# Two heads as one unit in a decode attention kernel: three slots of 64 KB a partition in place of five of 32 KB

## The chip, the core and the metric

The kernel runs on one core of a Trainium2 chip. The core has a matrix engine (PE, with its weight loads shown as PEld), a vector engine (DVE), an activation engine (ACT), GpSimd (POOL) and a queue engine (SP), and 16 DMA engines that move data between HBM and the on-chip SBUF of 128 partitions. Matrix products land in PSUM. The metric is the device time of one execution in microseconds.

## The reference

One decode step of a transformer block for B = 2 sequences, D = 512, H = 32 heads of 128 columns, a cache of 8192 keys and values for each head, and a gated feed-forward part of F = 1792. Everything is float32.

```python
q = layernorm(x) @ wq                       # (2, 1, 512) @ (512, 4096), split into 32 heads
scores = einsum("bhqd,bhkd->bhqk", q, k_cache) * 128 ** -0.5
p = softmax(scores)
o = einsum("bhqk,bhkd->bhqd", p, v_cache)
h = x + concat_heads(o) @ wo                # (4096, 512)
y = layernorm(h)
out = h + (silu(y @ w_gate) * (y @ w_up)) @ w_down
```

k_cache and v_cache hold 268 MB each, and all else is small beside them: each byte is used once, with one query row for each head and sequence.

## The kernel before

**Work.** A unit is one head of one sequence, i = 0 to 63 (head `i // 2`, sequence `i % 2`). Its K is 8192 x 128 floats, 4 MB, laid out so that partition p holds 64 consecutive keys, one run of 32 KB. The scores are made on DVE: `mult` (L245) multiplies half of K, 128 x 4096, in place by the query row, and `reduce` (L248) adds over the 128 columns; two such pairs make a unit. `local_max` (L256) takes the largest score of a partition, `spread_max` (L260) turns the 128 of them into a row on PE, and `softmax`, called one unit later between the first `mult` and the first `reduce`, takes the largest of that row on DVE (L264), brings it to all partitions with a PE product and an ACT copy (L266, L268), takes the exponential with its row sums on ACT (L271) and sums them over the partitions on PE (L275). `recip` follows between the second pair. `pv` (L288) multiplies p by V: 16 products of 128 x 512, each on a 32-column strip of PE, four strips in turn; in the trace each is two matrix instructions. `epilogue` (L301, L304, L311) copies the four strips out of PSUM, adds them with weights 1/denominator and stores one column of `oT`.

**Slots and the load queue.** One pool of five slots of 32 KB a partition (`RING = 5`) holds everything that is loaded: K units, V units, wq and wo in four groups of eight heads each (2 MB a group), and at the end w_gate, w_up and w_down. `order` is the list of all loads; `pump` issues them in that order on SP, each as soon as the item five places before it in the list has been marked `used`. On the chip a load waits at the head of SP's queue for the last reader of its slot, and the loads behind it wait with it. `after[i]` says which V units are multiplied during K unit i: the lag between K and V grows from one unit to five (`LEAD`, `STEP`). w_q's next group is projected (`project_q`, L223) every 16 units, and wo's group is applied (`project_o`, L318) after each 16.

**Order of the work.** `manual_schedule` keeps the program's order on each engine. In a unit, PE runs the two softmax products of the unit before (L266, L275), then `pv` of the V unit that is due, then `spread_max`, then the epilogue.

Of the kernel before, what the change touches and what calls it, by code (L numbers as in the profile page):

```python
# [8 lines left out]
F32 = mybir.dt.float32  # L9
# [5 lines left out]
RING = 5  # L15
# [4 lines left out]
def tile_decode_block(  # L20
# [16 lines left out]
    assert DH == P and B == 2 and D == 512 and F == 14 * P  # L37
# [3 lines left out]
    NJ = S // P  # L41
    FINE = 16
    NCH = NJ // FINE
    G = 8
    NG = H // G
    NP = B * H
    LEAD = 4
    STEP = 12
# [3 lines left out]
    NW = NJ // W  # L52

# [3 lines left out]
    ring = ctx.enter_context(tc.tile_pool(name="ring", bufs=RING))  # L57
# [10 lines left out]


    def k_pieces(i):  # L70
        return NCH if i == 0 else 1

    def v_pieces(i):
        return NCH if i == NP - 1 else 1

    def pieces(kind, i):
        n = k_pieces(i) if kind == "k" else v_pieces(i)
        return [((kind, i), e * (NJ // n), NJ // n) for e in range(n)]


    after = []
    for i in range(NP):
        upto = i - 1 - min(LEAD, i // STEP)
        after.append(list(range(sum(map(len, after)), upto + 1)))
    rest = list(range(sum(map(len, after)), NP))

    order = [(("wq", 0), 0, 1)]

    def stream_v(i):
        if i == NP - 2:  # L90
            order.append((("wo", NG - 1), 0, 1))
        order.extend(pieces("v", i))
        if (i + 1) % (B * G) == 0 and i + 1 < NP:
            order.append((("wo", i // (B * G)), 0, 1))

    for i in range(NP):
        g, r = divmod(i + 2, B * G)
        if r == 0 and g < NG:
            order.append((("wq", g), 0, 1))
        order.extend(pieces("k", i))  # L100
        for v in after[i]:
            stream_v(v)
    for v in rest:
        stream_v(v)
    order += [(("wg", 0), 0, DC)] + [(("wu", 0), c, n) for c, n in ((0, 2), (2, 1), (3, 1))]
    order += [(("wd", 0), c, n) for c, n in ((0, 4), (4, 4), (8, 3), (11, 2), (13, 1))]
    items = list(dict.fromkeys(o[0] for o in order))
# [4 lines left out]
    def load(item, e, n):  # L112
        if item not in slot:
            slot[item] = ring.tile([P, NJ * DH], F32, name="ring")
        t = slot[item]
        kind, i = item
        if kind in "kv":
            src = k_cache if kind == "k" else v_cache
            h, b = divmod(i, B)
            nc.sync.dma_start(  # L120
                t[:, e * DH : (e + n) * DH],
                src[b, h].rearrange("(p j) d -> p (j d)", p=P)[:, e * DH : (e + n) * DH],
            )
        elif kind == "wq":
            nc.sync.dma_start(
                t[:, : DC * G * DH].rearrange("p (c m) -> p c m", c=DC),
                wq[:, i * G * DH : (i + 1) * G * DH].rearrange("(c p) m -> p c m", p=P),
            )
        elif kind == "wo":
            nc.sync.dma_start(  # L130
                t[:, : G * D].rearrange("p (c m) -> p c m", c=G),
                wo[i * G * DH : (i + 1) * G * DH, :].rearrange("(c p) m -> p c m", p=P),
            )
        elif kind in ("wg", "wu"):
            src = w_gate if kind == "wg" else w_up
            nc.sync.dma_start(
                t[:, e * F : (e + n) * F],
                src.rearrange("(p c) f -> p (c f)", p=P)[:, e * F : (e + n) * F],
            )
        else:  # L140
            nc.sync.dma_start(
                t[:, e * D : (e + n) * D],
                w_down.rearrange("(p c) m -> p (c m)", p=P)[:, e * D : (e + n) * D],
            )

    def pump():
        while state["next"] < len(order):
            piece = order[state["next"]]
            if piece[0] not in slot:
                n = items.index(piece[0])  # L150
                if n >= RING and items[n - RING] not in done:
                    return
# [11 lines left out]
    ones = const.tile([P, P], F32, name="ones")  # L164
    nc.vector.memset(ones, 1.0)
    nscale = const.tile([1, P], F32, name="nscale")
    nc.vector.memset(nscale, -SCALE)
    mhalf = const.tile([B, 1], F32, name="mhalf")
    nc.vector.memset(mhalf, -0.5)
    opart = []  # L170
    for n in range(2):
# [3 lines left out]

    diag = const.tile([P, W], F32, name="diag")
    nc.vector.tensor_reduce(
        diag, ident.rearrange("p (t r) -> p r t", t=4)[:, :W, :], axis=AX.X, op=OP.add
    )
# [8 lines left out]
    def layernorm(src, runs):  # L188
# [8 lines left out]
        y = work.tile([B, D], F32, name="ln_y")  # L197
        nc.vector.tensor_scalar(y, src, mv[:, 0:1], rstd, op0=OP.subtract, op1=OP.mult)
        yt = psum.tile([P, DC, B], F32, name="small", bufs=3)
        for c in range(DC):  # L200
            cols = y.rearrange("b (p c) -> b c p", c=DC) if runs else y.rearrange("b (c p) -> b c p", c=DC)
            nc.tensor.transpose(yt[:, c, :], cols[:, c, :], ident[:B, :B])
# [3 lines left out]
    xT_ps = layernorm(xs, False)  # L206
    xT = const.tile([P, DC, B], F32, name="xT")
    nc.vector.tensor_copy(xT, xT_ps)
    xb = const.tile([P, DC * B, P], F32, name="xb")
    nc.vector.tensor_copy(  # L210
        xb, xT.rearrange("p c b -> p (c b)")[:, :, None].to_broadcast([P, DC * B, P])
    )

    qsb = {}

    def project_q(g):
        w = slot[("wq", g)][:, : DC * G * DH].rearrange("p (c m) -> p c m", c=DC)
        qsb[g] = work.tile([P, B, G * DH], F32, name="qsb")
        for b in range(B):
            for n in range(0, G * DH, 512):  # L220
                ps = psum.tile([P, 512], F32, name="wide", bufs=2)
                for c in range(DC):
                    nc.tensor.matmul(  # L223
                        ps,
                        xb[:, c * B + b, :],
                        w[:, c, n : n + 512],
                        start=(c == 0),
                        stop=(c == DC - 1),
                    )
                nc.scalar.activation(qsb[g][:, b, n : n + 512], ps, AF.Copy)  # L230
        used(("wq", g))
# [6 lines left out]
    def mult(i, j0, n):  # L238
        h, b = divmod(i, B)
        g, hh = divmod(h, G)  # L240
# [3 lines left out]
        qb = qsb[g][:, b, hh * DH : (hh + 1) * DH][:, None, :].to_broadcast([P, n, DH])  # L244
# [17 lines left out]
    def softmax(i):  # L262
        gm = work.tile([1, 1], F32, name="gm")
        nc.vector.tensor_reduce(gm, st[i]["mrow"], axis=AX.X, op=OP.max)  # L264
        nb_ps = psum.tile([P, 1], F32, name="small", bufs=3)
        nc.tensor.matmul(nb_ps, nscale, gm, start=True, stop=True)  # L266
        nb = work.tile([P, 1], F32, name="nb")
        nc.scalar.activation(nb, nb_ps, AF.Copy)  # L268
        st[i]["p"] = work.tile([P, NJ], F32, name="p", bufs=LEAD + 4)
        rs = work.tile([P, 1], F32, name="rs")  # L270
        nc.scalar.activation(  # L271
            st[i]["p"], st[i]["s"], AF.Exp, bias=nb, scale=SCALE, accum_out=rs
        )
        st[i]["den"] = psum.tile([P, 1], F32, name="small", bufs=3)
        nc.tensor.matmul(st[i]["den"], ones, rs, start=True, stop=True)  # L275

    def recip(i):
        r = work.tile([P, 1], F32, name="r")
        nc.vector.reciprocal(r, st[i]["den"])  # L279
        st[i]["r"] = work.tile([P, W], F32, name="rdiag", bufs=LEAD + 4)  # L280
        nc.scalar.activation(st[i]["r"], diag, AF.Copy, scale=r)  # L281

    def pv(i, j0, n):
        vt = slot[("v", i)]
        o = opart[i % 2]
        for w in range(j0 // W, (j0 + n) // W):
            t = w % 4
            nc.tensor.matmul(  # L288
                o[32 * t : 32 * t + W, :],
                st[i]["p"][:, w * W : (w + 1) * W],  # L290
# [7 lines left out]
    def epilogue(i):  # L298
        h, b = divmod(i, B)
        osb = work.tile([P, W * DH], F32, name="osb")  # L300
        nc.scalar.activation(osb, opart[i % 2], AF.Copy)  # L301
        ot_ps = psum.tile([P, 1], F32, name="small", bufs=3)
        for a in range(W):
# [3 lines left out]
                st[i]["r"][:, a : a + 1],  # L307
# [3 lines left out]
        nc.scalar.activation(oT[:, h, b : b + 1], ot_ps, AF.Copy)  # L311
        del st[i]

    def project_o(h0, h1):
        g = h0 // G
        w = slot[("wo", g)][:, : G * D].rearrange("p (c m) -> p c m", c=G)
        for h in range(h0, h1):
            nc.tensor.matmul(  # L318
                attn, oT[:, h, :], w[:, h - g * G, :], start=(h == 0), stop=(h == H - 1)
            )  # L320
        if h1 % G == 0:
            used(("wo", g))

    def values(v):
        pv(v, 0, NJ)

    def outputs(v):
        epilogue(v)
        if (v + 1) % (B * G) == 0 and v + 1 < NP:
            project_o((v + 1) // B - G, (v + 1) // B)  # L330

    project_q(0)
    for i in range(NP):
        n = FINE if k_pieces(i) > 1 else 2 * FINE
        for c, j0 in enumerate(range(0, NJ, n)):
            mult(i, j0, n)
            if i:
                if c == 0:
                    softmax(i - 1)
                if c == 1:  # L340
                    recip(i - 1)
            reduce(i, j0, n)
            if c == 1:
                for v in after[i]:
                    values(v)
        if (i + 1) % (B * G) == 0 and i + 1 < NP:
            project_q((i + 1) // (B * G))
        local_max(i)

        if i == NP - 1:  # L350
            for v in after[i]:
                outputs(v)
            for v in rest[:2]:
                values(v)
                outputs(v)
        spread_max(i)
        if i < NP - 1:
            for v in after[i]:
                outputs(v)
    softmax(NP - 1)  # L360
    warm = const.tile([1, 1], F32, name="warm")
    nc.scalar.activation(warm, mhalf[:1, :], AF.Sigmoid)
    recip(NP - 1)
    for v in rest[2:-1]:
        values(v)
        outputs(v)
        if v == NP - 3:
            project_o(H - G, H - 1)
    for j0 in range(0, NJ, FINE):
        pv(NP - 1, j0, FINE)  # L370
    epilogue(NP - 1)
    project_o(H - 1, H)


    h1 = const.tile([B, D], F32, name="h1")
    nc.vector.tensor_add(h1, attn, xs)  # L376
    hT_ps = layernorm(h1, True)
# [99 lines left out]
```

## Time and profile before

| | us |
|---|---|
| median of 3 runs | 1319.63 (1319.53 to 1319.73) |
| the profiled execution, its own time | 1319.64 |
| its span | 1317.8 |
| DVE busy | 1156.5 |
| PE busy | 662.0 |
| PE weight loads busy | 255.4 |
| ACT busy | 117.2 |

The span runs from the first instruction to the last; the execution's own time is 1.84 us longer. A group of instructions is given by line, engine, operation and tiles, with its count, busy time, mean duration and the idle time of its engine just before it. A DMA issue is shown with the median time from issue to landing. In the rows by time, the columns are start, duration, engine, line, operation, tiles, and in brackets the idle time before with what ended it; "SPq" is the queue engine issuing a load. In the rows by window the columns are the window, its length, the busy time (and number of instructions) of PE, PEld, DVE, ACT and POOL, PE's granted clock as a share of full speed, the busy share of the DMA engines, and GB/s.

### The profile page before, as it was taken

The page shows a single profiled execution, that of the slowest core. Times are in us where ns is not written, and L with a number is a line of the kernel's source. Part 1 is how long each engine was busy: PE and PEld are TensorE (multiplying, and loading weights), DVE is VectorE, ACT ScalarE, POOL GpSimd, SP SyncE. Part 2 cuts the span into 40 slices and gives each one's busy share as a digit, 9 for nine tenths or more (in the row PEclk, how much of TensorE's full clock was granted, in tenths as well). Part 3 has the DMA queues.
Part 4 walks back from the last instruction along what each step waited for, and adds up shares of the span by engine and source line. Part 5 has one row for each costly group of instructions (what it writes and reads, how often), then busy time and mean ns, then how long its engine had stood idle before and what let it go on. Part 6 is the DMA issues. An engine that isn't in the chain of part 4 may idle for free.

```text
span 1317.8 us, 8050 instructions
## 1 busy us (share of the span) xinstructions
PE 662.0 (50%) x3328; PEld 255.4 (19%) x3328; DVE 1156.5 (88%) x474; ACT 117.2 (9%) x404; POOL 1.9 (0%) x9
## 2 busy tenths in 40 slices
PE   5444444257554434535753444442644753444586
PEld 2121111113211111211321122111212211111122
DVE  6999999997999999989889999997799999999601
ACT  1001000001000000000100000000100000100010
POOL 0000000000000000000000000000000000000000
PEclk9666656567675756666767656656857756665677
DMA  9999999999999999999999999999999999999997
GB/s 402 438 433 428 430 437 435 422 439 432 428 433 437 433 430 430 436 432 434 429 430 430 435 436 430 433 429 434 436 430 429 432 430 431 437 435 431 429 425 334
DMA packets 26921, 565.19 MB, mean 429 GB/s; under 512 B 2426, under 2 KB 2434, under 8 KB 9220
## 3 DMA queue, kind: packets, MB, share of 16 engines
q1 hardware_dynamic: 26872, 564.67, 99.7%
q8 instruction: 26, 0.43, 0.1%
q14 instruction: 11, 0.09, 0.0%
q10 hardware_dynamic: 12, 0.01, 0.0%
HBM read 564.66 MB, written 0.00 MB: 428 GB/s over the span
## 4 chain that ended last, share of the span: by engine, by line
DVE 47%; DMA 45%; PE 7%; issue 0%; ACT 0%; SPq 0%; DVEq 0%
DMA ring<-in_A_k_cache_dram 31%; DVE s L248 24%; DVE ring L245 23%; DMA ring<-in_A_v_cache_dram 11%; PE wide L223 4%; DMA ring<-in_B_w_down_dram 2%; PE opart L288 2%; PE attn L318 1%; DMA ring<-in_A_wq_dram 1%; DVE m L256 0%; PE small L425 0%; PE small L304 0%; DVE r L279 0%; PE small L260 0%; DVE gm L264 0%
## 5 line engine op out<-in xcount | busy, mean ns | idle before, releaser
L245 DVE TENSOR_TENSOR ring<-ring,qsb 128x4096 f32<-128x4096 f32 (+1 forms) x130 | 565.5, 4350 | 69.6 <-DMA ring<-in_A_k_cache_dram 57.7
L248 DVE TENSOR_REDUCE s<-ring 128x32 f32<-128x4096 f32 (+1 forms) x130 | 565.1, 4347 | 0.7 <-DVE gm L264 0.5
L288 PE MATMUL opart<-ring,p 128*4 128x512 f32 x2048 | 356.3, 858 | 110.1 <-DMA ring<-in_A_v_cache_dram 110.1
L260 PE MATMUL small<-ident,m 128*1 128x128 f32 x128 | 31.7, 341 | 270.9 <-DVE m L256 270.9
L266 PE MATMUL small<-gm,nscale 1*128 1x1 f32 x128 | 35.9, 347 | 203.6 <-DVE gm L264 203.6
L288 PEld LDWEIGHTS opart<-ring,p 128*4 128x4 f32 x2048 | 58.3, 108 | 349.2 <-issue 232.6
L304 PE MATMUL small<-rdiag,osb 128*128 128x1 f32 x512 | 98.1, 313 | 7.1 <-ACT osb L301 7.1
L304 PEld LDWEIGHTS small<-rdiag,osb 128*128 128x128 f32 x512 | 92.7, 271 | 32.4 <-issue 18.7
L266 PEld LDWEIGHTS small<-gm,nscale 1*128 1x128 f32 x128 | 30.5, 294 | 213.5 <-DVE gm L264 210.8
L260 PEld LDWEIGHTS small<-ident,m 128*1 128x1 f32 x128 | 5.5, 81 | 329.2 <-DVE m L256 327.0
L275 PE MATMUL small<-rs,ones 128*128 128x1 f32 x128 | 36.2, 352 | 47.0 <-ACT p L271 47.0
L223 PE MATMUL wide<-ring,xb 128*128 128x512 f32 x128 | 58.2, 614 | 3.1 <-DMA ring<-in_A_wq_dram 3.1
L281 ACT ACTIVATE rdiag<-diag,r 128x4 f32<-128x4 f32 x64 | 19.0, 297 | 452.3 <-DVE r L279 452.3
L264 DVE TENSOR_REDUCE gm<-small 1x1 f32<-1x128 f32 x64 | 17.4, 272 | 35.1 <-PE small L260 35.1
L301 ACT ACTIVATE osb<-opart 128x512 f32<-128x512 f32 x64 | 37.8, 590 | 92.3 <-PE opart L288 92.3
L275 PEld LDWEIGHTS small<-rs,ones 128*128 128x128 f32 x128 | 30.8, 298 | 52.4 <-ACT p L271 52.4
L268 ACT ACTIVATE nb<-small 128x1 f32<-128x1 f32 x64 | 10.9, 171 | 286.0 <-PE small L266 285.6
L318 PE MATMUL attn<-ring,oT 128*2 128x512 f32 x64 | 36.2, 726 | 0.3 <-ACT oT L311 0.3
L311 ACT ACTIVATE oT<-small 128x1 f32<-128x1 f32 x64 | 11.0, 171 | 279.1 <-PE small L304 279.1
L223 PEld LDWEIGHTS wide<-ring,xb 128*128 128x128 f32 x128 | 24.8, 196 | 35.8 <-issue 35.8
L376 DVE TENSOR_TENSOR h<-attn,xs 2x512 f32<-2x512 f32 x1 | 0.7, 679 | 29.2 <-PE attn L318 29.2
L271 ACT ACTIVATE p<-s,nb 128x64 f32<-128x64 f32 x64 | 22.2, 348 | 2.1
(43 smaller groups left out, 88.4 us busy)
## 6 DMA issues: line engine op xcount, KB each, us to landing
ring<-in_A_k_cache_dram SPq DMA_DIRECT2D x63, 4096.0 KB, 32.4
ring<-in_A_v_cache_dram SPq DMA_DIRECT2D x63, 4096.0 KB, 30.5
ring<-in_A_wq_dram SPq DMA_DIRECT2D x4, 2048.0 KB, 26.0
ring<-in_A_wo_dram SPq DMA_DIRECT2D x4, 2048.0 KB, 27.0
ring<-in_A_k_cache_dram SPq DMA_DIRECT2D x4, 1024.0 KB, 12.3
ring<-in_A_v_cache_dram SPq DMA_DIRECT2D x4, 1024.0 KB, 23.0
ring<-in_B_w_gate_dram SPq DMA_DIRECT2D x1, 3584.0 KB, 33.5
ring<-in_B_w_down_dram SPq DMA_DIRECT2D x2, 1024.0 KB, 27.4
```

Source lines behind the costliest of these rows:

```text
L223: nc.tensor.matmul(ps, xb[:, c * B + b, :], w[:, c, n : n + 512], start=(c == 0), stop=(c == DC - 1),)
L245: nc.vector.tensor_tensor(kt, kt, qb, op=OP.mult)
L248: nc.vector.tensor_reduce(st[i]["s"][:, j0 : j0 + n], k_view(i, j0, n), axis=AX.X, op=OP.add)
L260: nc.tensor.matmul(st[i]["mrow"], st[i]["m"], ident, start=True, stop=True)
L266: nc.tensor.matmul(nb_ps, nscale, gm, start=True, stop=True)
L271: nc.scalar.activation(st[i]["p"], st[i]["s"], AF.Exp, bias=nb, scale=SCALE, accum_out=rs)
L275: nc.tensor.matmul(st[i]["den"], ones, rs, start=True, stop=True)
L281: nc.scalar.activation(st[i]["r"], diag, AF.Copy, scale=r)
L288: nc.tensor.matmul(o[32 * t : 32 * t + W, :], st[i]["p"][:, w * W : (w + 1) * W], vt[:, w * W * DH : (w + 1) * W * DH], start=(w < 4), sto ...
L301: nc.scalar.activation(osb, opart[i % 2], AF.Copy)
L304: nc.tensor.matmul(ot_ps, osb[:, a * DH : (a + 1) * DH], st[i]["r"][:, a : a + 1], start=(a == 0), stop=(a == W - 1),)
L318: nc.tensor.matmul(attn, oT[:, h, :], w[:, h - g * G, :], start=(h == 0), stop=(h == H - 1))
```

## The change

- A unit is two neighbouring heads of one sequence (m = 0 to 15, `i = 2 m + b`), so there are 32. Head 2m lies on partitions 0 to 63, head 2m + 1 on 64 to 127, and a partition holds 128 consecutive keys: one run of 64 KB, 8 MB a load. DVE's instructions are on 128 x 8192 except in unit 0, and there are as many of them for each unit as there were before.
- The five slots become three of 64 KB a partition: two for K (`kslot`) and one for V (`vslot`). wq (8 MB, rows `(p c)`, runs of 64 KB) is loaded whole as the first load, into V's slot; K unit 0 comes in four pieces behind it. wo (8 MB, runs of 2 KB) is loaded whole into a K slot after V unit 30 and before V unit 31. w_gate and w_up share a K slot, w_down goes to V's slot.
- The list of loads is wq, K0, K1, V0, K2, V1, K3, V2, ... K31, V30, wo, V31, w_gate and w_up, w_down, all still on SP in this order. A load is issued when its own slot's last user is done.
- `softmax` serves both heads: the maximum is taken over two halves of the row, there are two bias products (64 columns each), two exponentials on 64 partitions each, written into `pz`, a zeroed stationary tile of 8 columns in which each head fills its own 4, and one denominator product with a block matrix `sides`.
- `pv` has 32 products for a unit with 8 stationary columns instead of 4; two `pz` tiles and two PSUM tiles alternate. The epilogue writes two columns of `oT`.
- `pv(i - 2)` and its epilogue are called in unit i, behind the second `reduce` in the program and so behind `softmax(i - 1)` on PE. In the last unit `pv(30)` follows too.
- `project_q` runs once, over all heads, with the two heads of a pair on the two 64-column halves of PE: 64 products, 128 instructions, as many as in the four groups before. `project_o` runs once for 30 heads on four strips; the last two heads and x are added behind it.
- Several small tiles of the last stage move into a free part of w_up's slot; GpSimd's descriptor scratch is made smaller.

```diff
-RING = 5
...
+    HP = P // 2
+    NJ = S // HP
+    U = B * H // 2
+    MQ = H // 2
+    HALF = (slice(0, HP), slice(HP, P))
...
+    BUFS = {"kslot": 2, "vslot": 1}
+    HOME = {"k": "kslot", "v": "vslot", "wq": "vslot", "wo": "kslot", "wf": "kslot", "wd": "vslot"}
...
+    order = [(("wq", 0), 0, 1)] + pieces("k", 0)
+    for i in range(1, U):
+        order += pieces("k", i) + pieces("v", i - 1)
+    order += [(("wo", 0), 0, 1)] + pieces("v", U - 1)
+
+    order += [(("wf", 0), c, n) for c, n in ((0, DC), (DC, 2), (DC + 2, 1), (DC + 3, 1))]
...
             nc.sync.dma_start(
                 t[:, e * DH : (e + n) * DH],
-                src[b, h].rearrange("(p j) d -> p (j d)", p=P)[:, e * DH : (e + n) * DH],
+                src[b, 2 * m : 2 * m + 2].rearrange("h (p j) d -> (h p) (j d)", p=HP)[
+                    :, e * DH : (e + n) * DH
+                ],
             )
...
     def pump():
         while state["next"] < len(order):
             piece = order[state["next"]]
             if piece[0] not in slot:
-                n = items.index(piece[0])
-                if n >= RING and items[n - RING] not in done:
+                name = HOME[piece[0][0]]
+                n = items[name].index(piece[0])
+                if n >= BUFS[name] and items[name][n - BUFS[name]] not in done:
                     return
             load(*piece)
             state["next"] += 1
...
     def softmax(i):
-        gm = work.tile([1, 1], F32, name="gm")
-        nc.vector.tensor_reduce(gm, st[i]["mrow"], axis=AX.X, op=OP.max)
+        gm = work.tile([1, 2], F32, name="gm")
+        nc.vector.tensor_reduce(
+            gm, st[i]["mrow"].rearrange("p (k r) -> p k r", k=2), axis=AX.X, op=OP.max
+        )
         nb_ps = psum.tile([P, 1], F32, name="small", bufs=3)
-        nc.tensor.matmul(nb_ps, nscale, gm, start=True, stop=True)
+        for k in range(2):
+            nc.tensor.matmul(nb_ps[HALF[k]], nscale, gm[:, k : k + 1], start=True, stop=True)
         nb = work.tile([P, 1], F32, name="nb")
         nc.scalar.activation(nb, nb_ps, AF.Copy)
...
+        for k, h in enumerate(HALF):
+            nc.scalar.activation(
+                pz[i % 2][h, :, k * W : (k + 1) * W],
+                st[i]["s"][h].rearrange("p (w a) -> p w a", a=W),
+                AF.Exp,
+                bias=nb[h],
+                scale=SCALE,
+                accum_out=rs[h],
+            )
...
         for w in range(j0 // W, (j0 + n) // W):
             t = w % 4
             nc.tensor.matmul(
-                o[32 * t : 32 * t + W, :],
-                st[i]["p"][:, w * W : (w + 1) * W],
+                o[32 * t : 32 * t + 2 * W, :],
+                pz[i % 2][:, w, :],
                 vt[:, w * W * DH : (w + 1) * W * DH],
...
+    project_q()
+    for i in range(U):
+        n = NJ // 4 if i == 0 else NJ // 2
         for c, j0 in enumerate(range(0, NJ, n)):
             mult(i, j0, n)
-            if i:
-                if c == 0:
-                    softmax(i - 1)
-                if c == 1:
-                    recip(i - 1)
+            if i and c == 0:
+                softmax(i - 1)
+            if i and c == 1:
+                recip(i - 1)
             reduce(i, j0, n)
-            if c == 1:
-                for v in after[i]:
-                    values(v)
-        if (i + 1) % (B * G) == 0 and i + 1 < NP:
-            project_q((i + 1) // (B * G))
+        if i >= 2:
+            values(i - 2)
         local_max(i)
+        if i == U - 1:
+            values(U - 2)
         spread_max(i)
...
-    nc = _bacc.Bacc("TRN2", target_bir_lowering=False, num_devices=1)
+    nc = _bacc.Bacc("TRN2", target_bir_lowering=False, num_devices=1, dynamic_dma_scratch_size=2048)
```

More of the change, by code (lines that the diff above doesn't have):

```diff
@@ L310, in epilogue @@
             )
-        nc.scalar.activation(oT[:, h, b : b + 1], ot_ps, AF.Copy)
+        nc.scalar.activation(oT[:, 2 * m : 2 * m + 2, b], ot_ps, AF.Copy)
         del st[i]
[L314 to L317, printed above, removed]
-            nc.tensor.matmul(
-                attn, oT[:, h, :], w[:, h - g * G, :], start=(h == 0), stop=(h == H - 1)
-            )
-        if h1 % G == 0:
-            used(("wo", g))
@@ L324, in values, with wo_rows, project_o @@
[L324 to L334, printed above, removed]
+    def values(i):
+        pv(i, 0, NJ)
+        epilogue(i)
+    def wo_rows(h):
+        return slot[("wo", 0)][:, h * D : (h + 1) * D]
+    def project_o():
+        ps = psum.tile([P, D], F32, name="wide", bufs=2)
+        nc.vector.memset(ps, 0.0)
+        for h in range(H - 2):
+            t = h % 4
+            nc.tensor.matmul(
+                ps[32 * t : 32 * t + B, :],
+                oT[:, h, :],
+                wo_rows(h),
+                start=(h < 4),
+                stop=(h >= H - 6),
+            )
+        acc = work.tile([P, D], F32, name="osb", bufs=1)
+        nc.scalar.activation(acc, ps, AF.Copy)
+        nc.tensor.matmul(attn, ident[:B, :B], xs, start=True, stop=False)
+        nc.tensor.matmul(attn, diag[:, :B], acc, start=False, stop=False)
@@ L360, in tile_decode_block @@
-    softmax(NP - 1)
+    softmax(U - 1)
     warm = const.tile([1, 1], F32, name="warm")
     nc.scalar.activation(warm, mhalf[:1, :], AF.Sigmoid)
[L363 to L377, printed above, removed]
+    recip(U - 1)
@@ L378, in tile_decode_block @@
+    project_o()
+    for _, j0, n in pieces("v", U - 1):
+        pv(U - 1, j0, n)
+    epilogue(U - 1)
+    for h in (H - 2, H - 1):
+        nc.tensor.matmul(attn, oT[:, h, :], wo_rows(h), start=False, stop=(h == H - 1))
+    used(("wo", 0))
+    rest = slot[("wf", 0)][:, 2 * DC * F :]
+    h1 = rest[:B, :D]
+    nc.scalar.activation(h1, attn, AF.Copy)
+    hT_ps = layernorm(attn)
     nc.vector.tensor_copy(hT[:, :, :B], hT_ps)
@@ L431, in tile_decode_block @@
             )
-    used(("wd", 0))
-    res = const.tile([P, P], F32, name="res")
+    res = rest[:, D + 3 * FQ : D + 3 * FQ + P]
     nc.vector.tensor_copy(res, f_ps)
```

179 lines of the change are left out of this document (69 added, 110 removed).

## The prediction

> **What bounds the kernel now.** I read the page first: span, engines, DMA rows, the chain of waits.
>
> ```profile
> span 1317.8 us, 8050 instructions
> PE 662.0 (50%) x3328; PEld 255.4 (19%) x3328; DVE 1156.5 (88%) x474; ACT 117.2 (9%) x404; POOL 1.9 (0%) x9
> DMA  9999999999999999999999999999999999999997
> GB/s 402 438 433 428 430 437 435 422 439 432 428 433 437 433 430 430 436 432 434 429 430 430 435 436 430 433 429 434 436 430 429 432 430 431 437 435 431 429 425 334
> q1 hardware_dynamic: 26872, 564.67, 99.7%
> DVE 47%; DMA 45%; PE 7%; issue 0%; ACT 0%; SPq 0%; DVEq 0%
> ```
>
> The DMA engines are busy in every slice but the last, and SP's queue q1 moves 564.67 MB through them without a hole. The bound is the stream; DVE at 88% runs close beside it, which is why the chain names both. What keeps the stream whole is shown by the issues, by SP's waits, and by the rate in three windows:
>
> ```profile
> ring<-in_A_k_cache_dram SPq DMA_DIRECT2D x63, 4096.0 KB, 32.4
> ring<-in_A_v_cache_dram SPq DMA_DIRECT2D x63, 4096.0 KB, 30.5
> ```
> ```profile
> SPq L120 <- DVE m L256: 942.1, 60, 18.1
> SPq L120 <- PE opart L288: 97.6, 9, 17.3
> ```
> ```profile
> 33.00:100.00 67.00, 30.86 (x160) 12.43 (x164) 66.84 (x27) 5.42 (x21) 0.00 (x0) 0.65 1.01 434
> 100.00:600.00 500.00, 236.05 (x1168) 92.37 (x1164) 465.69 (x183) 43.40 (x156) 0.00 (x0) 0.64 1.00 432
> 600.00:1200.00 600.00, 302.54 (x1454) 116.94 (x1450) 557.79 (x220) 53.92 (x191) 0.00 (x0) 0.66 1.00 432
> 1261.00:1280.00 19.00, 17.17 (x87) 4.90 (x90) 0.45 (x2) 3.23 (x9) 0.00 (x0) 0.82 1.00 419
> ```
>
> A load of 4.19 MB takes 9.7 us at 432 GB/s, but lands 32.4 us after its issue: for 22.7 us it stands behind loads issued earlier. That lead is the cover. SP waits about 1,000 us for a reader to free a slot, up to 18 us at a time, and no DMA engine notices, since more than two loads are always under way.
>
> **What the change does to that cover.** The bytes stay the same, so every gain or loss is a hole in the stream opened or closed. Take SP's list: ..., K(i), V(i-1), K(i+1), V(i). V(i-1) needs the only V slot, so it waits for the last product of pv(i-2). That is called in unit i, and on PE it stands behind softmax(i-1), whose maximum DVE takes only after the first `mult` of unit i, so after K(i) has landed. But K(i) is the last load issued: behind it SP holds V(i-1), and behind that K(i+1), although K(i+1)'s slot was freed when unit i-1's last `reduce` ended. So when K(i) lands nothing is in flight, and the stream stands still until pv(i-2) ends. Then V(i-1) and K(i+1), 16.78 MB, flow, and unit i+1 begins when K(i+1) lands. The second K slot buys nothing here. This is a closed loop from K(i) landing to K(i+1) landing, and its length is the period of a unit. Its terms come from these rows:
>
> ```profile
> L245 DVE TENSOR_TENSOR ring<-ring,qsb 128x4096 f32<-128x4096 f32 x126 | 556.4, 4416 | 60.9 <-DMA ring<-in_A_k_cache_dram 57.7 <-ACT qsb L230 3.2
> L248 DVE TENSOR_REDUCE s<-ring 128x32 f32<-128x4096 f32 x126 | 556.0, 4412 | 0.5 <-DVE gm L264 0.5
> L288 PE MATMUL opart<-ring,p 128*4 128x512 f32 x2048 | 356.3, 858 | 110.1 <-DMA ring<-in_A_v_cache_dram 110.1
> L245 DVE TENSOR_TENSOR ring<-ring,qsb 128x2048 f32<-128x2048 f32 x4 | 9.1, 2284 | 8.7 <-ACT qsb L230 8.7
> ```
> ```profile
> 639.52 5.31 PE L288 MATMUL opart<-ring,p 128*4 128x512 f32 x32
> 644.89 0.33 SPq L120 DMA_DIRECT2D ring<-in_A_v_cache_dram  x1
> 649.85 4.42 DVE L245 TENSOR_TENSOR ring<-ring,qsb 128x4096 f32<-128x4096 f32 x1
> 654.51 0.58 PE L266 MATMUL small<-gm,nscale 1*128 1x1 f32 x2 [2.14 <-DVE gm L264]
> 655.33 0.35 ACT L271 ACTIVATE p<-s,nb 128x64 f32<-128x64 f32 x1
> 655.58 0.19 ACT L271 ACTIVATION_READ_ACCUMULATOR p<-s,nb 128x1 f32 x1
> 655.82 0.58 PE L275 MATMUL small<-rs,ones 128*128 128x1 f32 x2 [0.73 <-ACT p L271]
> 656.34 6.05 PE L288 MATMUL opart<-ring,p 128*4 128x512 f32 x32
> 657.15 0.15 PEld L288 LDWEIGHTS opart<-ring,p 128*4 128x4 f32 x4 [0.70 <-issue]
> 661.36 0.10 PEld L288 LDWEIGHTS opart<-ring,p 128*4 128x4 f32 x4 [0.65 <-issue]
> 667.74 4.42 DVE L245 TENSOR_TENSOR ring<-ring,qsb 128x4096 f32<-128x4096 f32 x1
> 699.10 3.62 PE L288 MATMUL opart<-ring,p 128*4 128x512 f32 x32 [0.63 <-DMA ring<-in_A_v_cache_dram]
> 699.53 0.11 PEld L288 LDWEIGHTS opart<-ring,p 128*4 128x4 f32 x4 [0.32 <-issue]
> ```
> ```profile
> 0.73 0.44 SPq L125 DMA_DIRECT2D ring<-in_A_wq_dram  x1
> 8.35 7.15 PE L223 MATMUL wide<-ring,xb 128*128 128x512 f32 x11 [3.09 <-DMA ring<-in_A_wq_dram]
> 12.75 0.20 PEld L223 LDWEIGHTS wide<-ring,xb 128*128 128x128 f32 x1 [0.52 <-issue]
> 13.62 0.19 PEld L223 LDWEIGHTS wide<-ring,xb 128*128 128x128 f32 x1 [0.24 <-issue]
> 14.05 0.19 PEld L223 LDWEIGHTS wide<-ring,xb 128*128 128x128 f32 x1 [0.24 <-issue]
> 14.25 0.60 ACT L230 ACTIVATE qsb<-wide 128x512 f32<-128x512 f32 x1 [11.63 <-PE wide L223]
> 14.88 2.29 DVE L245 TENSOR_TENSOR ring<-ring,qsb 128x2048 f32<-128x2048 f32 x1 [8.69 <-ACT qsb L230]
> ```
>
> 1. First `mult`, 128 x 8192. 2284 ns for 2048 columns and 4416 for 4096 make 2132 ns for each 2048 more: 4416 + 2 x 2132 = 8680, 8.68 us.
> 2. From its end over the maximum to PE: 654.51 - 649.85 - 4.42 = 0.24 us.
> 3. Softmax chain on PE and ACT: 656.34 - 654.51 = 1.83 us, and now a second bias pair (0.58, L266's row) and a second exponential with its sum (0.35 + 0.19): 2.95 us. If the second ones hide entirely, 1.83; if each exponential doubles with its 128 columns, 3.65. I take 2.95, the rows' own durations one after the other.
> 4. pv, 64 instructions in 16 rounds of four. A round takes 0.84 us at half clock (657.15 to 661.36, five rounds) and 0.43 at full (699.10 to 699.53). PE comes out of a long idle stretch every time, so it starts slow: it went fast 6.85 us after its first product in one row (654.51 to 661.36) and 4.4 in another (8.35 to 12.75). The chain uses up 2.95 of that. 3.9 slow us are 4.6 rounds, and 11.4 fast ones take 4.9: 8.8 us; 1.45 slow us are 1.7 rounds, and 14.3 take 6.1: 7.6. With a last drain of some 0.3 us I take 8.6. Bounds: all fast 2 x 3.62 = 7.2, all slow 16 x 0.84 = 13.4.
> 5. Product to SP's issue: 644.89 - (639.52 + 5.31) = 0.06 us.
> 6. Two loads: 16.78 MB at 432 GB/s = 38.84 us. With 439 and 402 (best slice of the page, and worst but the last) 38.2 and 41.7.
> 7. What a load costs beyond its bytes when nothing is in flight: the first one, 2.10 MB, is issued at 0.73 and starts PE at 8.35, so 7.62 - 4.85 = 2.77 us. It could be as low as 2, as those were short runs.
>
> Sum: 8.68 + 0.24 + 2.95 + 8.6 + 0.06 + 38.84 + 2.77 = 62.14 us, against 2 x 17.89 = 35.8 (649.85 to 667.74) for two heads when DVE paced the kernel, and 38.84 when the stream does. DVE needs 4 x 8.68 + 0.23 = 34.95 us of a unit (0.23 is 17.89 less its four long instructions, two of L245's and two of L248's), so it idles 27 us and binds nowhere.
>
> The Trainium skill (DMA: Bandwidth & Descriptors, section Anatomy of one DMA) fits a GpSimd-issued load by 2.0 us plus its bytes over 436 GB/s; by that, an estimate, terms 6 and 7 would be 40.5 us instead of 41.6, and the whole 33 us shorter. This queue's first load shows 2.77 where the page has 2.0, so the sum keeps the row.
>
> **Start.** wq is 8.39 MB, 19.42 us: landed at 0.73 + 2.77 + 19.42 = 22.9. From there to DVE's start 14.88 - 8.35 = 6.5 us passed, and do again if the two 64-column halves run together, as pv's strips do (four in 0.43 us, the time of one L223 product, 13.62 to 14.05). DVE starts at 29.5, works 8 x 4.41 us on unit 0, and ends at 65.0; K1 is there by 61.8. Unit 1 ends at 100.1. `project_q` is done at 22.9 + 5.9 + 7 x 8 x 0.43 = 52.9, before the stream reaches V0, so V0 and K2 follow without a hole: K2 lands at 0.73 + 2.77 + 5 x 19.42 = 100.6. If the halves take turns, the projection ends near 80, and everything comes 21 us later.
>
> **End.** K31 lands at 100.6 + 29 x 62.14 = 1902.7. From there: V30 is issued at +20.5 and has flowed at +41.7; wo, free to go, follows until +61.7 (419 GB/s); pv(30) ends by +52.3, so V31 follows at once until +81.1; w_gate and w_up (7.34 MB, their slot free at +35) until +98.6, w_down (3.67 MB, pv(31) done by +84) until +107.4, landed +108.4. The tail after the last piece:
>
> ```profile
> 1310.48 4.10 PE L425 MATMUL small<-ring,gT 128*32 128x128 f32 x80 [1.10 <-DMA ring<-in_B_w_down_dram]
> 1314.65 0.29 DVE L434 COPY res<-small 128x128 f32<-128x128 f32 x1 [6.40 <-PE small L425]
> ```
>
> From the copy to the span's end are 3.15 us, and only the last 8 of those products wait for the last piece (0.4 us): the end is at +112.0. wo's one projection (30 heads) and the feed-forward's arithmetic lie under the loads of this stretch; without that cover the former would cost some 6 to 13 us. Span 2014.7; with the 1.84 us around it, 2016.5. The profiled execution's time, 1319.64, is the median of the runs (1319.63), so nothing is converted.
>
> Edits at nothing: two `pz` tiles for `p`, fewer instructions on DVE and ACT, the epilogue for two heads, tiles moved at the end, GpSimd's added clears: all lie in the 27 us that DVE and ACT idle, or under the first load. The epilogue and the next `spread_max` follow pv on PE while 38 us of loads run.
>
> **Rivals.**
> - *The stream stays whole* (other side). If SP could pass the waiting V(i-1), or pv(i-2) were done before K(i) landed, the time would be 564.67 MB at 432 GB/s (1307.1) + 2.77 + 0.73 + the tail 3.6 + 1.84 = 1316, at 434 GB/s 1310: same or faster. For it: fewer, longer loads, and 34.95 us of DVE fit into 38.84. Against it: one V slot, one queue, and pv(i-2) behind softmax(i-1). It decides only if the hold of 20.5 us (terms 1 to 5) falls to about nothing. 3%.
> - *PE stays slow all through pv.* For it: the granted clock of 0.64 to 0.66 in the windows, and runs such as 6.05 us for half as many products. Against: each such run ends fast. 13.4 instead of 8.6 us: 29 x 4.8 = 139 more, 2156. 10%.
> - *Rows of 64 KB flow slower.* No load here has that pitch. At 402 GB/s: 29 x 2.9 plus 8 at both ends = 92 more, 2108. Against: 32 KB rows run at 432 without a sign of it. 9%. The Trainium skill (DMA: Bandwidth & Descriptors, section Latency and other measured facts) reports copies slowing at large power-of-two row pitches, 207 against 214 GB/s at 512 KiB and half at 4 MiB; it speaks against this edit, though far above 64 KB, and no run here shows it.
> - *The change does not do what it says*, in that 64 KB runs are cut up again: then nothing moves, since 32 KB runs gave the rates used here.
>
> **How the numbers follow.** The loop as summed has 78%; its own range is 1945 (pv all fast, 2.0 us of latency, 435 GB/s) to 2055 (halves in turn, longer exponentials). The range 1945 to 2110 takes in the slow rows, and leaves out the slow clock and the whole stream. A change under 0.2% could not be told from none here. Slower 0.97, faster 0.02, same 0.01, the last two from the first rival.
>
> **What would show it.** Right: DMA share near 65% with about 280 GB/s over the span; the loads of K landing every 62 us; DVE waiting some 27 us for K in each unit (about 800 in all) and busy near 57%; SP waiting for pv before each V, and K issued within half a microsecond behind it; K's time from issue to landing near 41 us and V's near 22. Term 4 is read from pv's duration in a unit, term 7 from V's 22 us less 19.4. Wrong: DMA share still over 95%, or V loads issued before the first product of their unit's softmax.

## The result

| | us |
|---|---|
| before, median of 5 runs | 1319.73 (1319.53 to 1320.09) |
| changed, median of 5 runs | 2001.87 (1999.09 to 2004.31) |
| ratio | 1.516, 95% interval 1.514 to 1.519 |
| forecast | 2016, range 1945 to 2110 |

The profiled execution took 2002.05 us with a span of 2000.0. The page of the changed kernel (span, engines, DMA share and rate in 40 slices, SP's queue):

```profile
span 2000.0 us, 6736 instructions
PE 451.6 (23%) x2948; PEld 158.7 (8%) x2948; DVE 1131.6 (57%) x249; ACT 76.8 (4%) x270; POOL 2.9 (0%) x14
DMA  9955567655577555775556765557755577655688
GB/s 419 421 231 231 252 294 336 273 231 250 253 336 315 231 231 252 315 336 252 231 231 294 336 288 236 231 252 336 315 248 235 231 315 336 253 249 211 294 346 379
q1 hardware_dynamic: 15640, 564.67, 66.4%
issue 99%; PE 1%; DVE 0%; POOL 0%; POOLq 0%
```

SP's queue moves the same 564.67 MB as before, but keeps the engines busy for 66% of the span instead of all of it. From the third slice to the third from the end, the DMA row shows fives to sevens. PE, DVE and ACT are all less busy than before (451.6, 1131.6 and 76.8 us, against 662.0, 1156.5 and 117.2), so none of them has taken over as the bound by more work. The last row, the chain of waits, is of no use here: it puts 99% down to "issue", that is, to time for which it shows no wait. One unit in order of time shows more:

```profile
962.07 8.69 DVE L230 TENSOR_TENSOR kslot<-kslot,qsb 128x8192 f32<-128x8192 f32 x1 [26.43 <-DMA kslot<-in_A_k_cache_dram]
971.00 0.37 PE L254 MATMUL small<-gm,nscale 1*64 1x1 f32 x4 [34.63 <-DVE gm L249]
973.19 9.03 PE L283 MATMUL opart<-vslot,pz 128*8 128x512 f32 x64
982.29 0.33 SPq L99 DMA_DIRECT2D vslot<-in_A_v_cache_dram  x1
982.71 0.38 SPq L99 DMA_DIRECT2D kslot<-in_A_k_cache_dram  x1
996.91 0.29 DVE L241 TENSOR_REDUCE m<-s 128x1 f32<-128x128 f32 x1
1023.46 8.69 DVE L230 TENSOR_TENSOR kslot<-kslot,qsb 128x8192 f32<-128x8192 f32 x1 [26.27 <-DMA kslot<-in_A_k_cache_dram]
```

K has landed at 962.07 and the first `mult` starts. Softmax of the unit before starts on PE at 971.00, pv at 973.19. When pv ends, at 982.22, SP issues V, and 0.42 us later K. K lands at 1023.46. DVE has finished its unit at 997.2 and waits 26.3 us. Two windows of that unit, before and after the issue (window, length, busy time of the engines, PE's clock, DMA share, GB/s):

```profile
962.07:982.29 20.22, 9.92 (x70) 2.51 (x70) 20.22 (x4) 1.15 (x5) 0.00 (x0) 0.63 0.00 0
982.29:1023.46 41.17, 2.46 (x10) 1.90 (x10) 14.87 (x5) 0.96 (x3) 0.00 (x0) 0.56 0.96 408
```

For 20.22 us nothing moves (0 GB/s). The waits of DVE and SP and the issues show that the other units are much like this one:

```profile
DVE kslot L230 <- DMA kslot<-in_A_k_cache_dram: 767.5, 30, 28.2
SPq L99 <- PE opart L283: 1186.3, 30, 40.7
kslot<-in_A_k_cache_dram SPq DMA_DIRECT2D x31, 40.7
vslot<-in_A_v_cache_dram SPq DMA_DIRECT2D x31, 21.8
```

### The profile page after: what moved, and what is told of

It is laid out like the page before. It is cut to its first block, busy times and chain, and to the rows that moved or that the text cites. A ratio compares the mean times of both kernels' runs of the same rounds, so it can differ in the third digit from the quotient of the medians.

```text
span 2000.0 us, 6736 instructions
## 1 busy us (share of the span) xinstructions
PE 451.6 (23%) x2948; PEld 158.7 (8%) x2948; DVE 1131.6 (57%) x249; ACT 76.8 (4%) x270; POOL 2.9 (0%) x14
## 3 DMA queue, kind: packets, MB, share of 16 engines
q1 hardware_dynamic: 15640, 564.67, 66.4%
## 4 chain that ended last, share of the span: by engine, by line
issue 99%; PE 1%; DVE 0%; POOL 0%; POOLq 0%
PE wide L385 0%; PE small L413 0%; DVE opart L165 0%; DVE kslot L402 0%; DVE ln_y L185 0%; DVE kslot L408 0%; PE small L188 0%; POOLq L459 0%; PE small L372 0%; POOL ln_rstd L183 0%; DVE ln_stats L177 0%; POOL ident masks.py:199 0%; DVE kslot L421 0%; DVE diag L148 0%; POOL ident masks.py:197 0%
## 5 line engine op out<-in xcount | busy, mean ns | idle before, releaser
L230 DVE TENSOR_TENSOR kslot<-kslot,qsb 128x8192 f32<-128x8192 f32 (+1 forms) x66 | 556.1, 8426 | 791.1 <-DMA kslot<-in_A_k_cache_dram 767.5
L233 DVE TENSOR_REDUCE s<-kslot 128x64 f32<-128x8192 f32 (+1 forms) x66 | 555.8, 8421 | 0.1
L283 PE MATMUL opart<-vslot,pz 128*8 128x512 f32 x2048 | 290.4, 728 | 18.1 <-DMA vslot<-in_A_v_cache_dram 18.1
L299 PE MATMUL small<-rdiag,osb 128*128 128x2 f32 x256 | 58.1, 349 | 207.4 <-ACT osb L296 207.4
L299 PEld LDWEIGHTS small<-rdiag,osb 128*128 128x128 f32 x256 | 55.4, 319 | 237.9 <-ACT osb L296 237.9
L283 PEld LDWEIGHTS opart<-vslot,pz 128*8 128x8 f32 x2048 | 55.6, 102 | 222.9 <-issue 202.4
L245 PE MATMUL small<-ident,m 128*1 128x128 f32 x64 | 18.5, 391 | 221.0 <-DVE m L241 221.0
L209 PE MATMUL wide<-vslot,osb 128*64 128x512 f32 x128 | 30.4, 640 | 17.3 <-DMA vslot<-in_A_wq_dram 17.3
L268 PE MATMUL small<-rs,sides 128*128 128x1 f32 x64 | 18.6, 359 | 41.7 <-ACT pz L259 41.7
L259 ACT ACTIVATE pz<-s,nb 64x128 f32<-64x128 f32 x64 | 25.5, 399 | 1.5
L245 PEld LDWEIGHTS small<-ident,m 128*1 128x1 f32 x64 | 3.6, 80 | 223.6 <-issue 210.4
L296 ACT ACTIVATE osb<-opart 128x512 f32<-128x512 f32 x32 | 18.5, 578 | 37.5 <-PE opart L283 37.5
```

The lines of the kernel that those rows point to most:

```text
L209: nc.tensor.matmul(ps[HALF[k]], xb[:, c * B + b, :], w[:, c, k, m : m + 4, :], start=(c == 0), stop=(c == DC - 1),)
L230: nc.vector.tensor_tensor(kt, kt, qb, op=OP.mult)
L233: nc.vector.tensor_reduce(st[i]["s"][:, j0 : j0 + n], k_view(i, j0, n), axis=AX.X, op=OP.add)
L245: nc.tensor.matmul(st[i]["mrow"], st[i]["m"], ident, start=True, stop=True)
L259: nc.scalar.activation(pz[i % 2][h, :, k * W : (k + 1) * W], st[i]["s"][h].rearrange("p (w a) -> p w a", a=W), AF.Exp, bias=nb[h], scale=S ...
L268: nc.tensor.matmul(st[i]["den"], sides.rearrange("p w a -> p (w a)"), rs, start=True, stop=True)
```

## The experiments

The theory is the loop of the prediction: K(i) lands, the first of the unit's two `mult`s, softmax(i-1), pv(i-2), then V(i-1) and K(i+1) flow. The rivals are that one V slot is too few whatever the order, that rows of 64 KB flow slower, and that PE stays at half clock. All edits are to the changed kernel.

### pv ahead of softmax

```diff
         n = NJ // 4 if i == 0 else NJ // 2
+        if i >= 2:
+            values(i - 2)
         for c, j0 in enumerate(range(0, NJ, n)):
...
-        if i >= 2:
-            values(i - 2)
         local_max(i)
```

> Only the order on PE changes: the two calls for pv(i-2) and its epilogue stand at the top of unit i, ahead of softmax(i-1). Slots, list of loads and queue are those of the change. Theory (a loop from K landing over the half mult, softmax and pv to the next V and K loads): pv(i-2) can now run when V(i-2) has landed, 19 us before K(i) lands, so V(i-1) is issued while K(i) flows; the loop then spans two units (about 61.4 us for two), less than the 38.5 us a unit that the stream needs. 29 units lose 61.4 - 38.5 = 22.9 us each: 1305 to 1325 us. Rival A (one V slot is too few, whatever the order): within 100 us of 2000. Rival B (rows of 64 KB flow slower): no hole in the stream, but a rate well under 432 GB/s, so over 1380 us.

Measured: 1457.51 us, ratio to before 1.105 (1.102 to 1.107). That is 544 us less than the change, and still 132 us over the top of the range that the theory expected. Rival A is out. Rows of one stretch:

```profile
710.48 8.69 DVE L230 TENSOR_TENSOR kslot<-kslot,qsb 128x8192 f32<-128x8192 f32 x1 [8.07 <-DMA kslot<-in_A_k_cache_dram]
745.74 0.37 PE L245 MATMUL small<-ident,m 128*1 128x128 f32 x1 [24.08 <-DVE m L241]
746.12 8.98 PE L283 MATMUL opart<-vslot,pz 128*8 128x512 f32 x61
754.07 8.69 DVE L230 TENSOR_TENSOR kslot<-kslot,qsb 128x8192 f32<-128x8192 f32 x1 [8.47 <-DMA kslot<-in_A_k_cache_dram]
755.18 0.33 SPq L99 DMA_DIRECT2D vslot<-in_A_v_cache_dram  x1
796.48 8.69 DVE L230 TENSOR_TENSOR kslot<-kslot,qsb 128x8192 f32<-128x8192 f32 x1 [7.29 <-DMA kslot<-in_A_k_cache_dram]
```

The expectation had overlooked an instruction. On PE, pv(i-2) no longer stands behind softmax(i-1), but behind `spread_max(i-1)` (L245), which waits for the maximum (m, L241) behind unit i-1's last `reduce`. So V is issued 44.7 us after a K landed (710.48 to 755.18), and the K behind it lands 41.3 us later: 86.0 us for two units (710.48 to 796.48), 43.0 each (43.3 in the mean of units 2 to 31). The loop was the right picture, with the wrong head of PE's queue in it. Rival B is not decided by this run, since its stream has holes too.

### V's loads from another queue

```diff
+            queue = nc.scalar if kind == "v" else nc.sync
-            nc.sync.dma_start(
+            queue.dma_start(
```

> Only the queue of the V loads changes: they are issued from ACT, so that K(i+1) no longer stands behind a waiting V(i-1). The order on PE stays that of the change. Theory: K(i+1) is issued when unit i-1's last reduce ends, some 20 us before K(i)'s unit has its pv done; the hole is filled with K, and what is left is the loop of V alone (pv 9 us, latency 3 us, and V's 19.3 us plus what K takes beside it): 38.6 to 41 us a unit, 1315 to 1390 us. Rival A (one V slot is the cause by itself): a V load still starts only after pv, so near 2000. Rival C (half of the loss is the queue, half the slot): 1600 to 1700.

Measured: 1402.50 us, ratio 1.062 (1.061 to 1.064). With the order on PE untouched, 599 of the 682 us come back once K need not stand behind a waiting V. The mean period, from the starts of unit 2 (104.96) and unit 30 (1229.20), is 40.2 us, within the 38.6 to 41 expected; the time is 12.5 us over the range. Waits of PE, issues, and windows of the middle and the end:

```profile
PE opart L284 <- DMA vslot<-in_A_v_cache_dram: 774.8, 30, 32.8
kslot<-in_A_k_cache_dram SPq DMA_DIRECT2D x31, 32.6
vslot<-in_A_v_cache_dram ACTq DMA_DIRECT2D x31, 31.8
100.00:600.00 500.00, 139.83 (x968) 43.64 (x968) 445.29 (x90) 27.82 (x101) 0.00 (x0) 0.61 0.95 407
1360.00:1405.00 45.00, 35.00 (x330) 11.45 (x330) 5.10 (x11) 4.14 (x8) 0.54 (x1) 0.85 0.55 228
```

Now the loop of V alone binds: it takes 31.8 us to land because K flows beside it, and PE waits 775 us for it. The excess lies at the end: V31 waits for pv(30), the stream runs at 228 GB/s in the window of the last 45 us, and from the start of unit 31 to the end of the span it is 135.8 us, against 113.7 in the change.

### Quarters in place of halves

```diff
-        n = NJ // 4 if i == 0 else NJ // 2
+        n = NJ // 4
```

> One size changes: every unit multiplies and reduces K in four quarters of 128 x 4096 instead of two halves of 128 x 8192, so softmax(i-1) starts after 4.42 us of unit i instead of 8.69. Theory: term 1 of the loop falls by 4.27 us, and the period with it: 30 units x 4.27 = 128 us less, 1865 to 1885 us, though DVE gets more instructions. Rival (DVE or the stream's rate sets the period): no change, or some us slower.

Measured: 1892.48 us: 109 less than the change, where 128 were expected and the rival said none. The time is 7 us above the range.

```profile
970.08 4.43 DVE L230 TENSOR_TENSOR kslot<-kslot,qsb 128x4096 f32<-128x4096 f32 x1 [22.29 <-DMA kslot<-in_A_k_cache_dram]
976.94 9.80 PE L283 MATMUL opart<-vslot,pz 128*8 128x512 f32 x64
986.81 0.33 SPq L99 DMA_DIRECT2D vslot<-in_A_v_cache_dram  x1
```

The `mult` gives back 4.26 us, but pv takes 0.7 us more: 9.71 in the mean of this run's units that the trace shows in one row, 9.05 in the change's. From K's landing to V's issue it is 16.7 us instead of 20.2. The mean period of units 2 to 31 falls from 61.55 to 57.99 us, and 30 times 3.56 makes 107. So what DVE does before softmax is in the loop, less what pv adds; why PE stays slow longer here is left open.

### Softmax before the first `mult`

```diff
+        if i:
+            softmax(i - 1)
         for c, j0 in enumerate(range(0, NJ, n)):
             mult(i, j0, n)
-            if i and c == 0:
-                softmax(i - 1)
```

> softmax(i-1) is called ahead of the first mult of unit i, and pv(i-2) still follows it. Theory: terms 1 and 2 leave the loop, and so does the landing of K(i): pv(i-2) starts some 3 us after unit i-1's last reduce, V(i-1) is issued 35 + 1 + 3 + 9 = 48 us after K(i-1) landed, K(i+1) lands 41.2 us later, so 89.4 us for two units, 44.7 each: 1480 to 1500 us. Between the change (61.4 a unit) and a whole stream (38.5). Rival A (one V slot whatever the order): the hole of pv, softmax and latency stays in every unit, near 52 us, 1730.

Measured: 1502.02 us, ratio 1.138 (1.136 to 1.140), 2 us above the range.

```profile
959.66 8.69 DVE L230 TENSOR_TENSOR kslot<-kslot,qsb 128x8192 f32<-128x8192 f32 x1 [11.73 <-DMA kslot<-in_A_k_cache_dram]
998.07 9.25 PE L283 MATMUL opart<-vslot,pz 128*8 128x512 f32 x64
1007.39 0.33 SPq L99 DMA_DIRECT2D vslot<-in_A_v_cache_dram  x1
1049.87 8.69 DVE L230 TENSOR_TENSOR kslot<-kslot,qsb 128x8192 f32<-128x8192 f32 x1 [11.73 <-DMA kslot<-in_A_k_cache_dram]
```

47.7 us from landing to V's issue, 42.5 to the next landing but one: 90.2 us for two units, against 89.4 expected. The loop spans two units, and the hole is filled in part by the K already under way.

### Half of pv

```diff
-        for w in range(j0 // W, (j0 + n) // W):
+        for w in range(j0 // W, min((j0 + n) // W, NW // 2)):
...
-                stop=(w >= NW - 4),
+                stop=(w >= NW // 2 - 4),
```

> Left out: the second half of the products of pv, so of the values only the first 64 keys of each partition count. All loads, softmax and DVE work stay. Theory (pv lies whole in the loop, on a PE that starts it at half clock): 8 rounds instead of 16; the rounds left out are the fast ones of 0.43 us, so pv falls from 9.05 to about 5.6 us, the period by 3.4, and the time by some 30 x 3.4 = 105 us: 1890 to 1905 us. Rival (PE hidden under the loads): 2000, no change. Rival (PE at half clock all through): 6.8 us a unit less, 1800.

Measured: 1898.32 us, 104 less than the change and within the range. A typical pv:

```profile
982.38 5.65 PE L283 MATMUL opart<-vslot,pz 128*8 128x512 f32 x32
```

Half of pv takes 5.65 us, not half of 9.05: the half left out is the fast one. The mean period falls by 3.45 us (61.55 to 58.10), as the mean of pv does (9.05 to 5.60). So PE's work is not hidden, and PE does not stay at half clock.

### K in two loads

```diff
-        n = 4 if (kind, i) in (("k", 0), ("v", U - 1)) else 1
+        n = 4 if (kind, i) in (("k", 0), ("v", U - 1)) else 2 if kind == "k" else 1
```

> Only the K loads change: each unit's K comes as two loads of 4 MB (32 KB runs), so the first mult waits for the first half alone, and the second half flows while softmax and pv hold up V's load. Order on PE, slots and queue stay. Theory: the hole after K falls by the 9.6 us of the second half, from about 23 to 13 us a unit: period 61.5 - 9.6 = 51.9, 1705 to 1730 us; the remaining loss is still one hole in each unit. V's load (still 64 KB runs) keeps its 21.8 us from issue to landing. Rival (the rate of 64 KB rows is what costs): a few per cent at most, 1940 or more.

Measured: 1706.97 us, ratio 1.294 (1.291 to 1.296), within the range.

```profile
971.92 8.69 DVE L230 TENSOR_TENSOR kslot<-kslot,qsb 128x8192 f32<-128x8192 f32 x1 [16.16 <-DMA kslot<-in_A_k_cache_dram]
991.60 0.33 SPq L99 DMA_DIRECT2D vslot<-in_A_v_cache_dram  x1
1023.05 8.69 DVE L230 TENSOR_TENSOR kslot<-kslot,qsb 128x8192 f32<-128x8192 f32 x1 [16.01 <-DMA kslot<-in_A_k_cache_dram]
```

The period is 51.1 us here. From V's issue to the next `mult` it is 31.5 us instead of 41.2: the second half of K, 9.7 us, now flows during the hold. V's own load still takes 21.8 us in the median, as in the change.

### One K slot in place of two

```diff
-    BUFS = {"kslot": 2, "vslot": 1}
+    BUFS = {"kslot": 1, "vslot": 1}
```

> Only the number of K slots changes, from two to one: K(i+1) now waits for unit i's own last reduce. Order on PE, list of loads and queue are those of the change. Theory (the second K slot buys nothing in a unit): the last reduce ends 35 us after K(i) landed, V(i-1) is issued at 20.2 and flows until 41, so K(i+1) is still issued before V(i-1) has flowed and follows it without a hole; the period stays 61.5. What is lost lies at the ends: K1 waits for unit 0 (K2 lands near 142 instead of 101), and w_gate waits for wo's last use, which puts 15 to 25 us of it behind the end of pv(31): 2002 + 41 + 20 = 2055 to 2075 us. Rival (the two K slots overlap loads with DVE, as two slots are meant to): DVE's 35 us and K's 19.3 add up, 15 us or more a unit, over 2450.

Measured: 2054.96 us, 53 more than the change, at the lower edge of the range.

```profile
1002.43 8.69 DVE L230 TENSOR_TENSOR kslot<-kslot,qsb 128x8192 f32<-128x8192 f32 x1 [26.42 <-DMA kslot<-in_A_k_cache_dram]
1022.79 0.33 SPq L99 DMA_DIRECT2D vslot<-in_A_v_cache_dram  x1
1037.25 0.33 SPq L99 DMA_DIRECT2D kslot<-in_A_k_cache_dram  x1
1063.80 8.69 DVE L230 TENSOR_TENSOR kslot<-kslot,qsb 128x8192 f32<-128x8192 f32 x1 [26.25 <-DMA kslot<-in_A_k_cache_dram]
```

K is issued 14.5 us after V instead of 0.4, and lands at the same moment of the unit: the period is 61.4. With 64 KB a partition fewer, a unit costs the same. The 53 us lie at the two ends, where they were expected: unit 2 begins 41.7 us later than in the change (143.15 against 101.42), and from the start of unit 31 to the end of the span it takes 12.2 us more.

### pv in the unit of its own V's landing

```diff
-        if i >= 2:
-            values(i - 2)
+        if i >= 1:
+            values(i - 1)
         local_max(i)
-        if i == U - 1:
-            values(U - 2)
         spread_max(i)
```

> Only the place of pv changes, as in the first experiment, but now pv(i-1) is called in unit i, behind softmax(i-1) and ahead of spread_max(i), which in the first experiment still stood before pv(i-2) on PE and waited there for unit i-1's last reduce. Slots, list of loads and queue are those of the change. Theory: pv(i-1) starts when V(i-1) lands, 19.3 us after K(i), and ends 9 us later, before unit i's DVE work does; V(i) then waits in the list behind K(i+1), already flowing. No hole in the stream: 564.67 MB at 432 to 437 GB/s and some 10 us around it, 1302 to 1320 us, against 1457 in the first experiment and 1319.7 for the kernel before. Rival A (one V slot is too few): 1400 or more. Rival B (rows of 64 KB flow slower): the stream whole, but under 425 GB/s, 1340 us or more.

Measured: 1316.12 us (1315.57 to 1316.88, 7 runs), ratio to before 0.9973, interval 0.9962 to 0.9984, within the range expected. It is 686 us faster than the change, and 0.3% under the kernel before, which counts as the same here. The 1316 us that the prediction gave for its first rival, a whole stream, is what a whole stream takes here. The DMA row of its page, a window and one unit of this run:

```profile
DMA  9999999999999999999999999999999999999998
100.00:600.00 500.00, 151.92 (x1040) 47.53 (x1038) 454.65 (x90) 28.89 (x104) 0.00 (x0) 0.62 1.00 433
663.11 9.71 PE L283 MATMUL opart<-vslot,pz 128*8 128x512 f32 x64 [8.11 <-DMA vslot<-in_A_v_cache_dram]
672.89 0.33 SPq L99 DMA_DIRECT2D vslot<-in_A_v_cache_dram  x1
678.63 0.33 SPq L99 DMA_DIRECT2D kslot<-in_A_k_cache_dram  x1
682.49 8.69 DVE L230 TENSOR_TENSOR kslot<-kslot,qsb 128x8192 f32<-128x8192 f32 x1 [3.56 <-DMA kslot<-in_A_k_cache_dram]
721.08 8.69 DVE L230 TENSOR_TENSOR kslot<-kslot,qsb 128x8192 f32<-128x8192 f32 x1 [3.47 <-DMA kslot<-in_A_k_cache_dram]
```

pv starts when its V lands, at 663.11, and the next load into V's slot is issued at 672.89, 9.6 us before the K ahead of it in the list has landed (682.49). The DMA engines are busy in every slice. The units shown are 38.6 us apart (682.49 to 721.08), and 16.78 MB at the 433 GB/s of the window are 38.75. So the slots and the queue of the change are enough: one V slot keeps the stream whole once it is emptied while K flows. What a second V slot would do with the order of the change was not run. And rows of 64 KB flow at 433 GB/s where those of 32 KB flowed at 432, which rules rival B out.

## Why the prediction was right

**What bounds and what goes.** The prediction's reading held: loads queued ahead kept the stream of the kernel before whole, and the change takes that cover away. The changed kernel shows what was forecast: DMA share 66.4% (near 65 forecast), 283 GB/s over the span (280), DVE at 57% and waiting 767.5 us for K (about 800), K and V landing 40.7 and 21.8 us after their issue (41 and 22).

**The terms of the loop**, against the unit shown above:

| term | forecast | measured |
|---|---|---|
| 1 first `mult` | 8.68 | 8.69 |
| 2 maximum, to PE | 0.24 | 0.24 |
| 3 softmax chain | 2.95 | 2.19 |
| 4 pv | 8.6 | 9.03 |
| 5 to SP's issue | 0.06 | 0.07 |
| 6 and 7 two loads with latency | 41.61 | 41.17 |
| sum | 62.14 | 61.39 |

The sum was 0.75 us too long, and the misses partly cancel: term 3 was too long by 0.76 and terms 6 and 7 together by 0.44, term 4 too short by 0.43. Term 3 was the largest miss:

```profile
971.63 0.40 ACT L259 ACTIVATE pz<-s,nb 64x128 f32<-64x128 f32 x1
972.67 0.59 PE L268 MATMUL small<-rs,sides 128*128 128x1 f32 x2 [1.30 <-ACT pz L259]
```

Of the two additions, the second exponential cost what its row said (two with their sums, 971.63 to 972.67, take about 1.0 us). The second bias product cost nothing: all four instructions run in 0.37 us, and the first exponential starts 0.63 us after the first of them (971.00 to 971.63), against 0.82 before with one product (654.51 to 655.33). Term 4 was too low by 0.4; its mechanism, slow rounds and then fast ones, shows in PE's weight loads of that pv (the number in brackets is the idle time between two rounds of four):

```profile
976.57 0.15 PEld L283 LDWEIGHTS opart<-vslot,pz 128*8 128x8 f32 x4 [0.70 <-issue]
977.33 0.10 PEld L283 LDWEIGHTS opart<-vslot,pz 128*8 128x8 f32 x4 [0.60 <-issue]
```

PE went fast 6.3 us after its first product (971.00 to 977.33; the granted clock is 0.51 up to there and 1.00 from there to pv's end), nearer to the slower of the two rows that the prediction took a middle of. Terms 6 and 7 came out 0.4 lower than their 41.61. The Trainium skill's fit (DMA: Bandwidth & Descriptors, section Anatomy of one DMA) would have made 40.5 of them, an estimate, 0.7 too low. The row of the first load was the nearer.

**Start, end and sum.** The first `mult` of unit 2 and of unit 31:

```profile
101.42 8.69 DVE L230 TENSOR_TENSOR kslot<-kslot,qsb 128x8192 f32<-128x8192 f32 x1 [1.04 <-DMA kslot<-in_A_k_cache_dram]
1886.34 8.69 DVE L230 TENSOR_TENSOR kslot<-kslot,qsb 128x8192 f32<-128x8192 f32 x1 [27.36 <-DMA kslot<-in_A_k_cache_dram]
```

The start was 0.8 us later than forecast (101.42 against 100.6), so the two halves of the query projection do run together: it ended at 53.2, where 52.9 was forecast and near 80 if the halves took turns. 29 periods took 1784.9 us, 61.55 each, against 1802.1: 17.2 less. The end took 113.7 against 112.0. Together -14.7, which is the whole difference between the spans 2014.7 and 2000.0. The end came out for another reason than the one given:

```profile
1993.21 3.45 PE L413 MATMUL small<-vslot,kslot 128*32 128x128 f32 x112 [1.73 <-DVE kslot L408]
1996.23 0.16 PEld L413 LDWEIGHTS small<-vslot,kslot 128*32 128x32 f32 x8 [0.24 <-DMA vslot<-in_B_w_down_dram]
```

The last products waited for the feed-forward's own arithmetic (DVE, L408), which the prediction had put under the loads, and w_down's last piece cost at most the 0.24 us before the last eight weight loads. That both chains are of nearly the same length was luck.

**The rivals.** A whole stream was excluded by the order on PE, and the last experiment shows that changing this order alone is enough to have one. What the prediction named together, one V slot, one queue and one order, is three things: changing the queue alone wins back 599 of the 682 us, and changing the order alone all of them. PE was not slow through all of pv (9.03 against 13.4 us; half of it took 5.65). Rows of 64 KB cost nothing, at 433 GB/s against 432. The Trainium skill (DMA: Bandwidth & Descriptors, section Latency and other measured facts) reports slower copies at large row pitches from 512 KiB on; no run here has such a pitch. "The second K slot buys nothing" was tested and held for the period of a unit; at the two ends the slot was worth 53 us.

## What to carry to other kernels

When a change keeps the bytes and moves slots, write down for each load what must happen before it is issued, follow that through every in-order queue that it passes (the loads ahead of it on SP, and the products ahead of its last reader on PE), and close the loop: its length, divided by the units it spans, is a lower bound of the period whatever the engines' shares say. Ask of a slot by how much its release comes before the load ahead of it in the queue has landed: here the second K slot, free in time, was worth nothing to a unit behind a waiting V load (a period of 61.4 us in the units shown, with it and without it). Before buying slots, try moving the reader: here the place of pv in the program was worth 686 us.

## What was not expected

- A product that looks small and free, `spread_max`, held pv for a whole DVE unit in the first experiment: 43.0 us a unit instead of the 38.6 of the last one (units shown).
- The same 64 products of pv took 9.71 us in the mean with quarters and 9.05 with halves, 8.4 to 10 over the runs. It goes with how long PE stays slow after its first product (8.0 us in the unit shown of the quarters, 974.75 to 982.71, against 6.3); what sets that length is open.
- Two queues shared the stream at 407 GB/s with the engines 95% busy, and yet each load took 32 us to land: V, which was urgent, got no more than its share beside K, which was not.
